# Moving the feed-forward weights of a fused attention and feed-forward kernel from casting DMAs into the queue that loads q, k and v, with staging tiles, on-chip casts and a new issue order

## The chip, the cores and the metric

The kernel runs on one core of a Trainium2 chip. The metric is the device time of one execution in microseconds (us). A profiled execution gives a span 1.7 us shorter than the time; positions such as "at 38.4 us" count from the start of that span. TensorE is called PE in the profile, VectorE DVE, ScalarE ACT, GpSimd POOL, SyncE SP. Every comparison is between runs in the fast state, and each kernel's runs in one call lie within 0.9% of each other.

## The reference, cut to what matters

```python
# q, k, v: (4 batches, 8 heads, 768 positions, 64), float32
k_min, k_max = per chunk of 32 keys, over the chunk
ub   = sum(max(q * k_min, q * k_max))        # bound of each query against each of the 24 chunks
top  = the 6 chunks with the highest bound    # causal chunks only
attn = softmax(q k^T / 8, in those chunks, causal) @ v
x    = attn as (3072 tokens, 512)
h    = x @ w_in                               # w_in 512 x 2048, float32
out  = (h * clip(h + 3, 0, 6) / 6) @ w_out    # w_out 2048 x 512, float32
```

Sixteen head pairs (4 batches, 4 pairs each) go through attention. The tokens of a batch form two groups of 384, and the eight groups go through the two weight matrices. The feed-forward part of a batch needs all four head pairs of that batch, and weights; attention needs no weights.

## The kernel before

Every step is a short function, and one long list of tokens gives the order in which the functions are called. Each engine executes its own instructions in that order. `lk.3` loads the keys of pair 3, `lq` queries, `lv` values, `K`/`Q` transpose keys and queries on PE, `U` are the bounds, `T`/`t8`/`sel`/`L`/`mt` the top-6 selection and its mask, `S` scores, `ex` exponentials, `af` causal masks on GpSimd, `A`/`B` the product with the values, `H` a hidden block (eight matmuls), `O` a quarter of a projection (four matmuls), `xt` DMA transposes of attention output, `Z` warm-up matmuls on zeros, `wi`/`wo` the loads of a quarter of w_in or w_out, `vc` the cast of the values. The other names are copies, casts and reductions between these steps, and the stores.

The loads and the weights, which the change is about:

```python
KS = ring(4, [P, NBLK, 2, D], FP32, "KS")      # the same for QS and VS
PT = [ring(6, [P, 2, 512], BF16, f"PT{i}_") for i in range(3)]
WIN  = const.tile([P, KT, DFF], BF16, name="WIN")
WOUT = const.tile([P, FT, DMODEL], BF16, name="WOUT")

def load(dst, x, i):                            # q, k or v of one pair: two DMAs of 192 KB
    b, hp = divmod(i, NPAIR)
    for e in range(2):
        nc.sync.dma_start(dst[:, :, e, :], x[b, 2 * hp + e].rearrange("(j p) d -> p j d", p=P))

def load_win(c):                                # a DMA that casts fp32 to bf16 on its way
    w = DFF // 4
    nc.gpsimd.dma_start(WIN[:, :, c * w:(c + 1) * w], wi[:, :, c * w:(c + 1) * w])

def load_wout(c):
    nc.gpsimd.dma_start(WOUT[:, 4 * c:4 * c + 4, :], wo[:, 4 * c:4 * c + 4, :])

def cast_v(i):
    nc.gpsimd.tensor_copy(VB[i % 4][:, :, :, 0:D], VS[i % 4][:])
```

The start of the order:

```
PRD PRA lk.0 lq.0 PRP PRL Z.b.10 lv.0 lk.1 lq.2 lq.1 lv.3 lv.2 lk.2 lq.3 lk.3 lv.1 Q.0.a lq.4 rp.0 rn.0 wi.1
qb.0 K.0.b wi.3 lk.4 kb.0 mx.0 wi.2 wi.0 mn.0 vc.0 U.0.c wo.1 lv.4 ub.0 K.1.a wo.0 T.0.x lk.5 kb.1 mx.1 wo.2
Q.2.b t8.0 wo.3 lq.6 rp.2 sel.0 qb.2 mn.1 Q.1.c L.0.y rn.2 lq.5 rp.1 rn.1 qb.1 vc.3 mt.0 U.1.a lv.7 S.0.1.b
... (cut: about 950 more tokens)
```

The softmax here doesn't subtract the row's maximum and nothing guards it: scores larger than these inputs give would overflow.

## Time and profile before

| | before |
|---|---|
| time, median of 3 runs | 325.63 us |
| span of the profiled execution | 323.6 us |
| PE busy | 288.9 us, 89% |
| first score matmul | 38.4 us |
| first hidden matmul | 73.4 us |

The view of stretches (windows) of the kernel before. After the stretch come its length and then, for each engine, busy us and the number of instructions; the last three columns are the granted PE clock (1.00 is full), the share of the DMA engines that was busy (a sum of packet times, which can pass 1), and GB/s moved.

```profile
0.00:10.00 10.00, 7.24 (x22) 3.76 (x22) 4.03 (x16) 2.68 (x4) 8.99 (x19) 1.00 0.99 175
10.00:20.00 10.00, 3.25 (x34) 2.20 (x34) 5.33 (x18) 1.77 (x3) 2.27 (x4) 0.67 1.21 195
20.00:30.00 10.00, 1.51 (x6) 1.14 (x6) 1.36 (x2) 1.34 (x2) 0.00 (x0) 0.50 1.22 196
30.00:40.00 10.00, 4.95 (x51) 3.01 (x53) 1.52 (x3) 2.19 (x4) 1.51 (x2) 0.50 1.26 217
40.00:50.00 10.00, 8.53 (x147) 6.49 (x145) 6.16 (x20) 8.30 (x11) 3.40 (x9) 0.97 1.09 214
...
60.00:80.00 20.00, 18.49 (x320) 13.68 (x319) 13.26 (x35) 16.33 (x21) 9.48 (x20) 1.00 0.78 161
...
120.00:200.00 80.00, 78.89 (x1005) 51.62 (x1002) 49.61 (x144) 56.89 (x75) 19.24 (x43) 1.00 0.35 77
200.00:324.00 124.00, 118.35 (x947) 65.82 (x943) 52.04 (x103) 56.42 (x74) 8.00 (x19) 1.00 0.17 47
```

PE is 17 us busy in the first 40 us, mostly at half clock, and nearly always busy from 60 us on. The DMA engines, on the other hand, are busy all through the first 50 us (shares of 0.99 to 1.26). The head is where PE waits.

PE's timeline in the head, kernel before: start us, duration us, engine, line, operation, output<-input, shapes, count, and in brackets the idle time just before it with what ended it.

```profile
24.59 1.51 PE L236 MATMUL PBb<-IDENT,QS 128*128 128x128 f32 x6 [7.81 <-DMA QS<-in_q_dram]
34.55 1.51 PE L236 MATMUL PBc<-IDENT,QS 128*128 128x128 f32 x6 [8.44 <-DMA QS<-in_q_dram]
35.86 0.45 PE L308 MATMUL PSy<-IDENTB,SEL 96*128 96x96 bf16 x3
38.41 0.39 PE L320 MATMUL PBb<-QB,KB 64*128 64x256 bf16 x2
```

L236 is the transpose of queries. Pair 2's queries arrive at 24.6 and pair 1's at 34.5, each after 8 us of waiting. The line after them, L308, is the mask transpose of pair 0, whose input was finished at 19.7 us; it stands behind the late transposes in PE's order. Only then do the scores (L320) start.

The list of DMA issues on the page of the kernel before (queue, count, KB each, median us from issue to landing):

```profile
QS<-in_q_dram SPq DMA_DIRECT2D x32, 192.0 KB, 3.9
WIN<-in_moe_w_in_dram POOLq DMA_DIRECT2D x4, 512.0 KB, 10.6
WOUT<-in_moe_w_out_dram POOLq DMA_DIRECT2D x4, 512.0 KB, 20.3
```

The size is what is written: 512 KB of bf16 for each 1 MB of fp32 read. Counting the DMA packet records of the trace by queue gives the clearest view of the collision. (This is a count made from the records, in stretches of 4 us; not a view of the profile. Durations are medians; the few 4 B records of each queue are left out of the counts.)

```
kernel before    q, k, v (SyncE queue)                    weights (GpSimd queue)
  4 to  8 us     3376 records of 256 B, 216 GB/s            14 records of 1 KB
 12 to 16 us      610 records,           39 GB/s, 31 ns    612 records, 157 GB/s, 96 ns
 24 to 28 us      626 records,           40 GB/s, 31 ns    607 records, 155 GB/s, 96 ns
 36 to 40 us     3453 records,          221 GB/s             0
```

As long as both queues have work, one record of each alternates. A weight record is four times as large as one of q, k or v and takes three times as long (96 against 31 ns), so equal turns leave q, k and v a fifth of the written bytes.

### The profile page before, as it was taken

Reading aid. Unit: us, or ns where it says so; the run is one execution under the profiler, and the core shown is the slowest. Engines: PE = TensorE matmul, PEld = TensorE weight load, DVE = VectorE, ACT = ScalarE, POOL = GpSimd, SP = SyncE. Lnnn points to the kernel's source line nnn. Section 1 sums busy time; section 2 is a strip of 40 time slices with the busy share of each in tenths; the row PEclk is TensorE's granted clock in tenths of the full one; section 3 lists DMA queues with packets and bytes.
Section 4 is the critical chain, followed back from the end, with each engine's and each line's share of the span. In section 5 each row is a group of like instructions: output and inputs, shape, how many; then the busy total and the mean of one; then the engine's idle time right before and its main releaser. Section 6 shows DMA issues by size and latency. Waiting matters only on the chain.

```text
span 323.6 us, 7386 instructions
## 1 busy us (share of the span) xinstructions
PE 288.9 (89%) x3058; PEld 178.6 (55%) x3058; DVE 168.6 (52%) x435; ACT 180.5 (56%) x234; POOL 61.5 (19%) x133
## 2 busy tenths in 40 slices
...
GB/s 173 193 196 196 223 214 210 218 173 99 49 149 187 120 104 173 137 34 79 146 22 53 34 34 66 49 0 34 67 65 35 50 51 50 66 34 65 2 65 66
DMA packets 92770, 32.21 MB, mean 100 GB/s; under 512 B 85568, under 2 KB 89664, under 8 KB 92736
## 3 DMA queue, kind: packets, MB, share of 16 engines
...
q8 instruction: 24, 0.39, 0.5%
...
## 4 chain that ended last, share of the span: by engine, by line
PE 75%; DMA 7%; DVE 7%; SPq 5%; ACT 4%; issue 1%; DVEq 0%; ACTq 0%
PE PSx L418 13%; PE PSy L418 12%; PE PBc L401 9%; PE PBb L401 8%; PE PBa L401 8%; DMA QS<-in_q_dram 6%; SPq L178 4%; DVE KM L258 4%; PE PSy L357 3%; PE PBa L236 2%; PE PBa L320 2%; PE PBc L320 2%; PE PBb L320 2%; PE PBc L236 2%; ACT KB L252 2%; PE PBa L328 2%
## 5 line engine op out<-in xcount | busy, mean ns | idle before, releaser
L401 PEld LDWEIGHTS <-WIN 128*128 128x128 bf16 x512 | 49.1, 98 | 33.8 <-issue 2.6
L341 POOL TENSOR_SCALAR_AFFINE_SELECT PT<-PT 128x256 bf16<-128x256 bf16 x96 | 38.1, 406 | 155.7 <-ACT PT L334 154.9
L418 PEld LDWEIGHTS <-GT 128*128 128x128 bf16 x384 | 35.8, 98 | 38.9 <-issue 1.1
L418 PE MATMUL PSx<-WOUT,GT 128*128 128x512 bf16 x208 | 49.6, 379 | 0.0
L418 PE MATMUL PSy<-WOUT,GT 128*128 128x512 bf16 x176 | 41.9, 379 | 0.0
L334 ACT ACTIVATE PT<-PBa 128x1024 bf16<-128x1024 f32 (+2 forms) x34 | 32.4, 953 | 4.3 <-PE PBa L328 4.3
L401 PE MATMUL PBc<-XT,WIN 128*128 128x384 bf16 x184 | 33.7, 326 | 1.2 <-DMA XT<-XB 1.2
L401 PE MATMUL PBb<-XT,WIN 128*128 128x384 bf16 x176 | 32.2, 326 | 0.4 <-DVE KM L258 0.4
L334 ACT ACTIVATE PT<-PBb 128x1024 bf16<-128x1024 f32 (+2 forms) x33 | 30.3, 918 | 4.0 <-PE PBb L328 4.0
L334 ACT ACTIVATE PT<-PBc 128x1024 bf16<-128x1024 f32 (+2 forms) x29 | 27.2, 938 | 8.1 <-PE PBc L328 8.1
L412 DVE SCALAR_TENSOR_TENSOR GT<-U,PBb 128x768 bf16<-128x768 bf16 x22 | 20.9, 950 | 16.3 <-PE PSx L418 9.5
L401 PE MATMUL PBa<-XT,WIN 128*128 128x384 bf16 x152 | 27.8, 326 | 0.0
L412 DVE SCALAR_TENSOR_TENSOR GT<-U,PBc 128x768 bf16<-128x768 bf16 x23 | 21.9, 950 | 10.3 <-ACT U L409 10.3
L409 ACT ACTIVATE U<-PBc 128x768 bf16<-128x768 f32 x23 | 18.7, 811 | 14.1 <-PE PBc L401 14.0
L357 PEld LDWEIGHTS <-PT 128*128 128x128 bf16 x672 | 23.9, 97 | 4.5 <-issue 1.2
L328 PEld LDWEIGHTS <-EM 64*128 64x128 bf16 x448 | 22.8, 96 | 5.6 <-issue 0.3
L412 DVE SCALAR_TENSOR_TENSOR GT<-U,PBa 128x768 bf16<-128x768 bf16 x19 | 18.1, 951 | 13.9 <-ACT U L409 13.6
L320 PEld LDWEIGHTS <-KB 64*128 64x128 bf16 x320 | 17.6, 95 | 12.4 <-issue 9.3
L409 ACT ACTIVATE U<-PBb 128x768 bf16<-128x768 f32 x22 | 17.9, 813 | 10.9 <-PE PBb L401 10.4
L409 ACT ACTIVATE U<-PBa 128x768 bf16<-128x768 f32 x19 | 15.4, 812 | 12.4 <-PE PBa L401 12.4
L426 ACT ACTIVATE OT<-PSx 128x512 f32<-128x512 f32 x13 | 7.8, 601 | 23.0 <-PE PSx L418 20.5
L231 POOL CAST VB<-VS 128x768 bf16<-128x768 f32 x16 | 13.1, 829 | 38.4 <-DMA VS<-in_v_dram 26.2
...
## 6 DMA issues: line engine op xcount, KB each, us to landing
KS<-in_k_dram SPq DMA_DIRECT2D x32, 192.0 KB, 4.0
QS<-in_q_dram SPq DMA_DIRECT2D x32, 192.0 KB, 3.9
VS<-in_v_dram SPq DMA_DIRECT2D x32, 192.0 KB, 4.2
...
WIN<-in_moe_w_in_dram POOLq DMA_DIRECT2D x4, 512.0 KB, 10.6
WOUT<-in_moe_w_out_dram POOLq DMA_DIRECT2D x4, 512.0 KB, 20.3
XT<-XB SPq DMA_TRANSPOSE x18, 2.8
```

The source lines that it names most:

```text
L178: nc.sync.dma_start(dst[:, :, e, :], x[b, 2 * hp + e].rearrange("(j p) d -> p j d", p=P))
L231: nc.gpsimd.tensor_copy(VB[i % 4][:, :, :, 0:D], VS[i % 4][:])
L236: nc.tensor.transpose(flat[:, j * P:(j + 1) * P], src[:, j].rearrange("p e d -> p (e d)"), IDENT32[:])
L320: nc.tensor.matmul(PSB[c][:, e, at:at + n], lhsT=K[rows, j * P:(j + 1) * P], rhs=Q[rows, q0:q0 + n], start=True, stop=q0 + n <= Q0, tile_p ...
L328: nc.tensor.matmul(PSB[c][:, e, at + lo - q0:at + hi - q0], lhsT=EM[rows, j, h, :], rhs=M[rows, lo - Q0 - HQ * h:hi - Q0 - HQ * h], start= ...
L334: nc.scalar.activation(PT[i % 3][u][:, :, 0:n], PSB[slot["S", i, u]][:, :, 0:n], ACT.Exp, scale=float(scale))
L341: nc.gpsimd.affine_select(out=T[:, :, lo:lo + P], in_=T[:, :, lo:lo + P], pattern=[[0, 2], [1, P]], compare_op=A.is_ge, fill=0.0, base=0, ...
L357: nc.tensor.matmul(O[:, e, t, :], lhsT=PT[i % 3][u][:, e, lo:lo + P], rhs=VB[i % 4][:, j, e, :], start=(j == 0), stop=(j == qb))
L401: nc.tensor.matmul(PSB[c][:, ff, 0:GRP], lhsT=WIN[:, kt, (2 * f + ff) * P:(2 * f + ff + 1) * P], rhs=XT[g % 3][:, kt, :], start=(kt == 0), ...
L409: nc.scalar.activation(slot["R", g, f][:], PSB[slot["H", g, f]][:, :, 0:GRP], ACT.Relu, bias=3.0)
L412: nc.vector.scalar_tensor_tensor(out=GT[g % 2][:, 2 * f:2 * f + 2, :], in0=slot["R", g, f][:], scalar=6.0, in1=PSB[slot["H", g, f]][:, :, ...
L418: nc.tensor.matmul(PSS[c][:], lhsT=GT[g % 2][:, f, t * P:(t + 1) * P], rhs=WOUT[:, f, :], start=(f == 0), stop=(f == FT - 1))
```

## The change

Its intent: bring the weights in when they are needed and not at the start, and let one queue decide the sequence of everything that is loaded. In the new path a chunk lands as fp32 in one of two staging slots and GpSimd casts it into the weight tile. To find the 16 KB per partition for the slots, the rings of staged q, k, v shrink from 4 to 3 and the tiles of exponentials are cut to the sizes that are used. The whole order is new.

```diff
-    KS = ring(4, [P, NBLK, 2, D], FP32, "KS")
+    KS = ring(3, [P, NBLK, 2, D], FP32, "KS")
     (the same for QS and VS, and in every use of them)
-    PT = [ring(6, [P, 2, 512], BF16, f"PT{i}_") for i in range(3)]
+    PT = [[const.tile([P, 2, sum(x[3] for x in unit)], BF16, name=f"PT{i}_{u}") for u, unit in enumerate(UNITS)]
+          for i in range(3)]
+    WS = ring(2, [P, 4, 512], FP32, "WS")
 
-    def load_win(c): ...        (casting DMA on nc.gpsimd, above)
-    def load_wout(c): ...
+    def load_w(n):
+        c = n % 4
+        nc.sync.dma_start(WS[n % 2][:], wi[:, :, 512 * c:512 * (c + 1)] if n < 4 else wo[:, 4 * c:4 * c + 4, :])
+
+    def cast_w(n):
+        c = n % 4
+        nc.gpsimd.tensor_copy(WIN[:, :, 512 * c:512 * (c + 1)] if n < 4 else WOUT[:, 4 * c:4 * c + 4, :], WS[n % 2][:])

 ORDER (wl = load_w, wc = cast_w)
-PRD PRA lk.0 lq.0 PRP PRL Z.b.10 lv.0 lk.1 lq.2 lq.1 lv.3 lv.2 lk.2 lq.3 lk.3 lv.1 Q.0.a lq.4 rp.0 rn.0 wi.1
-... (cut)
+PRD PRA lk.0 lq.0 PRP PRL Z.b.14 lk.1 lq.1 K.0.a lv.0 kb.0 mx.0 Q.0.b lv.1 mn.0 rp.0 lk.2 rn.0 qb.0 K.1.c lv.2
+U.0.a kb.1 lq.3 Q.1.b ub.0 lk.3 mn.1 T.0.x rp.1 qb.1 t8.0 lq.2 vc.0 lv.3 sel.0 rn.1 L.0.y vc.1 lk.4 mt.0 mx.1
+S.0.1.a S.0.3.b ex.0.1 wl.0 S.0.5.c ex.0.3 af.0.1 lq.4 U.1.a ex.0.5 S.0.4.b af.0.3 ub.1 T.1.x af.0.5 ex.0.4
+wl.1 S.0.0.a vc.2 ...
+... (cut; wl.2 and wl.3 stand beside lk.7 and lq.7, wl.4 to wl.7 in the first feed-forward stage)
```

More of the change, by code (lines that the diff above doesn't have):

```diff
@@ L34 @@
 ORDER = """
-PRD PRA lk.0 lq.0 PRP PRL Z.b.10 lv.0 lk.1 lq.2 lq.1 lv.3 lv.2 lk.2 lq.3 lk.3 lv.1 Q.0.a lq.4 rp.0 rn.0 wi.1
-qb.0 K.0.b wi.3 lk.4 kb.0 mx.0 wi.2 wi.0 mn.0 vc.0 U.0.c wo.1 lv.4 ub.0 K.1.a wo.0 T.0.x lk.5 kb.1 mx.1 wo.2
-Q.2.b t8.0 wo.3 lq.6 rp.2 sel.0 qb.2 mn.1 Q.1.c L.0.y rn.2 lq.5 rp.1 rn.1 qb.1 vc.3 mt.0 U.1.a lv.7 S.0.1.b
-ub.1 S.0.2.c ex.0.1 vc.2 S.0.3.a ex.0.2 S.0.5.b T.1.x af.0.1 lv.6 ex.0.3 S.0.4.c af.0.2 t8.1 ex.0.5 K.2.a
-af.0.3 sel.1 ex.0.4 af.0.5 S.0.0.b lk.6 mn.2 L.1.y kb.2 Q.3.c mx.2 B.0.0.x ex.0.0 lq.7 rn.3 U.2.a rp.3 af.0.0
@@ L40 @@
-mt.1 K.3.b qb.3 ub.2 S.1.2.a lk.7 kb.3 mn.3 S.1.3.c vc.1 ex.1.2 A.0.y mx.3 B.0.1.x lv.5 ex.1.3 na.0 af.1.2
-S.1.0.a S.1.1.b nb.0 T.2.y ex.1.0 af.1.3 U.3.c t8.2 ex.1.1 af.1.0 S.1.4.a ub.3 S.1.5.b af.1.1 ex.1.4 sel.2
-A.1.x L.2.y ex.1.5 Q.4.c na.1 mt.2 af.1.5 T.3.x lq.8 rp.4 rn.4 S.2.0.a qb.4 B.1.0.y t8.3 ex.2.0 S.2.3.b
-S.2.4.c sel.3 ex.2.3 af.2.0 S.2.1.a L.3.x B.1.1.y mt.3 ex.2.4 af.2.3 K.4.b nb.1 ex.2.1 S.3.3.c lk.8 mn.4 kb.4
-af.2.1 S.2.2.a mx.4 A.2.x ex.3.3 na.2 U.4.b ex.2.2 af.3.3 S.2.5.c ub.4 af.2.2 S.3.0.a ex.2.5 T.4.y S.3.5.b
@@ L45 @@
-ex.3.0 t8.4 af.2.5 S.3.4.c B.2.0.x ex.3.5 af.3.0 sel.4 B.2.1.x ex.3.4 af.3.5 L.4.y S.3.1.a nb.2 S.3.2.b ex.3.1
-mt.4 ex.3.2 af.3.1 S.4.5.c S.4.1.a A.3.x ex.4.5 af.3.2 S.4.4.b na.3 ex.4.1 af.4.5 S.4.2.c ex.4.4 X.0.1.y
-af.4.1 X.0.0.x vc.4 xe.0.1 S.4.0.a ex.4.2 S.4.3.b lv.8 xe.0.0 B.3.0.y ex.4.0 af.4.2 B.3.1.y ex.4.3 af.4.0
-H.0.6.c nb.3 af.4.3 A.4.x hu.0.6 H.0.7.a na.4 gt.0.6 K.5.b hu.0.7 H.0.5.c lk.9 mx.5 kb.5 gt.0.7 B.4.0.y hu.0.5
-B.4.1.y mn.5 H.0.4.a nb.4 H.0.2.b gt.0.5 hu.0.4 gt.0.4 H.0.0.c hu.0.2 gt.0.2 H.0.1.a hu.0.0 gt.0.0 X.1.0.x
@@ L50 @@
-hu.0.1 Q.6.b xe.1.0 H.0.3.c lq.10 rp.6 gt.0.1 qb.6 X.1.1.y rn.6 hu.0.3 Q.5.a xe.1.1 vc.7 O.0.0.0.x lq.9 rp.5
-rn.5 H.1.0.b qb.5 lv.11 gt.0.3 vc.6 U.5.a hu.1.0 lv.10 H.1.5.c ub.5 gt.1.0 T.5.y hu.1.5 H.1.2.a t8.5 H.1.6.b
-gt.1.5 hu.1.2 sel.5 H.1.3.c gt.1.2 hu.1.6 gt.1.6 K.7.a hu.1.3 O.0.0.1.x vc.5 lk.11 mx.7 kb.7 O.0.0.2.x lv.9
-mn.7 K.6.b gt.1.3 Q.7.a lk.10 kb.6 mn.6 L.5.y H.1.1.c lq.11 rp.7 mx.6 qb.7 O.0.0.3.x rn.7 hu.1.1 mt.5 U.6.b
-ot.0.0 gt.1.1 vc.8 S.5.5.a st.0.0 ub.6 S.5.3.c lv.12 ex.5.5 S.5.4.b T.6.y ex.5.3 af.5.5 O.1.1.0.x t8.6 ex.5.4
@@ L55 @@
-af.5.3 S.5.1.a S.5.2.c sel.6 ex.5.1 S.5.0.b ex.5.2 H.1.4.a af.5.1 ex.5.0 af.5.2 B.5.0.y hu.1.4 af.5.0 B.5.1.y
-Q.8.c gt.1.4 H.1.7.b lq.12 rp.8 nb.5 qb.8 rn.8 A.5.y hu.1.7 O.1.1.1.x na.5 O.1.1.2.x gt.1.7 L.6.y O.1.1.3.x
-mt.6 S.6.1.a ot.1.1 S.6.2.c S.6.0.b ex.6.1 st.1.1 vc.9 O.1.0.0.y ex.6.2 af.6.1 lv.13 O.1.0.1.y ex.6.0 af.6.2
-S.6.4.a af.6.0 S.6.5.c ex.6.4 S.6.3.b A.6.x ex.6.5 O.1.0.2.y na.6 ex.6.3 af.6.5 O.1.0.3.y af.6.3 K.8.a ot.1.0
-B.6.0.x lk.12 kb.8 mx.8 st.1.0 B.6.1.x K.9.c mn.8 vc.10 U.7.b lk.13 kb.9 nb.6 lv.14 U.8.a mn.9 O.0.1.0.y ub.8
@@ L60 @@
-O.0.1.1.y mx.9 T.8.x ub.7 Q.9.a t8.8 K.11.c lq.13 rp.9 sel.8 O.0.1.2.y lk.15 qb.9 rn.9 L.8.x O.0.1.3.y mt.8
-mx.11 S.8.1.b ot.0.1 S.8.5.a mn.11 T.7.x ex.8.1 st.0.1 O.0.2.0.y ex.8.5 af.8.1 t8.7 S.8.0.b af.8.5 S.8.3.a
-sel.7 ex.8.0 O.0.2.1.y ex.8.3 af.8.0 L.7.x U.9.b mt.7 af.8.3 A.8.x ub.9 S.8.2.a na.8 S.7.3.b ex.8.2 T.9.x
-O.0.2.2.y t8.9 ex.7.3 af.8.2 S.8.4.a af.7.3 sel.9 S.7.5.b ex.8.4 O.0.2.3.y ex.7.5 B.8.0.x B.8.1.x kb.11 af.7.5
-S.7.2.a nb.8 vc.12 ot.0.2 S.7.1.b S.7.4.c ex.7.2 st.0.2 L.9.y O.1.2.0.x mt.9 ex.7.1 af.7.2 ex.7.4 S.9.4.a
@@ L65 @@
-af.7.1 S.9.0.b ex.9.4 S.9.1.c B.7.0.y B.7.1.y ex.9.0 S.9.3.a nb.7 ex.9.1 af.9.0 S.9.5.b O.1.2.1.x xt.3 ex.9.3
-af.9.1 A.9.y ex.9.5 af.9.3 S.9.2.c na.9 af.9.5 S.7.0.a ex.9.2 K.10.b O.1.2.2.x ex.7.0 af.9.2 lk.14 mx.10
-K.12.c kb.10 af.7.0 mn.10 Q.10.a kb.12 mn.12 A.7.y lq.14 rp.10 H.3.4.b vc.11 na.7 qb.10 mx.12 xt.2 B.9.0.y
-lv.15 hu.3.4 B.9.1.y rn.10 H.3.2.c vc.13 gt.3.4 nb.9 H.3.5.a hu.3.2 gt.3.2 H.3.1.b hu.3.5 gt.3.5 H.3.3.c
-hu.3.1 gt.3.1 H.2.6.a hu.3.3 gt.3.3 H.2.2.b hu.2.6 gt.2.6 H.2.4.c hu.2.2 gt.2.2 H.2.3.a hu.2.4 gt.2.4 H.2.7.b
@@ L70 @@
-hu.2.3 gt.2.3 H.2.0.c hu.2.7 gt.2.7 H.2.5.a hu.2.0 gt.2.0 H.2.1.b hu.2.5 gt.2.5 U.10.c hu.2.1 Q.12.a ub.10
-gt.2.1 T.10.y rp.12 Q.11.c t8.10 qb.12 H.3.6.b lq.15 rp.11 sel.10 qb.11 O.1.2.3.x rn.12 hu.3.6 L.10.y rn.11
-U.12.a ot.1.2 mt.10 st.1.2 U.11.c gt.3.6 O.2.2.0.x ub.11 ub.12 T.11.y S.10.1.b t8.11 S.10.4.c ex.10.1 S.10.5.a
-ex.10.4 S.10.2.b af.10.1 sel.11 O.2.2.1.x ex.10.5 L.11.y ex.10.2 O.2.2.2.x af.10.5 mt.11 S.11.0.c af.10.2
-S.11.3.a ex.11.0 S.11.5.b O.2.2.3.x ex.11.3 af.11.0 T.12.y S.10.3.c ex.11.5 af.11.3 t8.12 S.11.2.a ot.2.2
@@ L75 @@
-af.11.5 S.10.0.b ex.10.3 sel.12 st.2.2 O.2.1.0.x ex.11.2 af.10.3 L.12.y O.2.1.1.x mt.12 ex.10.0 af.11.2
-B.10.0.y B.10.1.y af.10.0 S.12.1.c nb.10 S.12.2.a ex.12.1 S.12.3.b ex.12.2 af.12.1 S.12.0.c O.2.1.2.x ex.12.3
-af.12.2 O.2.1.3.x ex.12.0 af.12.3 S.12.4.a ot.2.1 af.12.0 S.12.5.b S.11.1.c ex.12.4 st.2.1 A.10.y A.12.x na.10
-vc.14 ex.12.5 Q.15.a na.12 ex.11.1 Q.13.b af.12.5 qb.15 af.11.1 B.12.0.y rn.13 A.11.x rp.13 H.3.0.c na.11
-qb.13 xt.4 K.13.b hu.3.0 B.12.1.y mx.13 kb.13 O.2.0.0.x gt.3.0 O.2.0.1.x mn.13 O.2.0.2.x nb.12 O.2.0.3.x
@@ L80 @@
-O.3.2.0.y ot.2.0 H.4.2.c st.2.0 H.4.3.b hu.4.2 gt.4.2 O.3.0.0.x hu.4.3 O.3.0.1.x gt.4.3 O.3.0.2.x U.13.c
-H.4.1.b ub.13 rp.15 rn.15 H.4.7.c hu.4.1 gt.4.1 H.3.7.a hu.4.7 gt.4.7 H.4.5.b hu.3.7 gt.3.7 H.4.4.c hu.4.5
-gt.4.5 O.3.0.3.x hu.4.4 H.4.0.a gt.4.4 ot.3.0 st.3.0 T.13.x hu.4.0 H.4.6.b t8.13 O.3.2.1.y sel.13 hu.4.6
-gt.4.0 L.13.x O.3.2.2.y mt.13 gt.4.6 S.13.3.c S.13.2.a ex.13.3 S.13.4.b O.4.0.0.x ex.13.2 af.13.3 O.3.2.3.y
-ex.13.4 af.13.2 S.13.1.c S.13.5.a ot.3.2 S.11.4.b ex.13.1 st.3.2 O.4.1.0.y ex.13.5 af.13.1 ex.11.4 O.4.1.1.y
@@ L85 @@
-af.13.5 O.4.1.2.y O.4.1.3.y K.15.c ot.4.1 K.14.a kb.15 mx.15 st.4.1 O.4.2.0.y kb.14 mn.15 O.4.2.1.y mn.14
-O.4.2.2.y mx.14 U.15.b S.13.0.c ub.15 O.4.2.3.y ex.13.0 O.4.0.1.x ot.4.2 af.13.0 st.4.2 T.15.y O.4.0.2.x t8.15
-O.4.0.3.x sel.15 Q.14.a ot.4.0 B.13.0.y rp.14 rn.14 st.4.0 L.15.x B.13.1.y qb.14 mt.15 U.14.b nb.13 S.15.4.c
-ub.14 S.15.0.a ex.15.4 S.15.3.b T.14.x ex.15.0 O.3.1.0.y t8.14 ex.15.3 O.3.1.1.y af.15.0 sel.14 O.3.1.2.y
-af.15.3 O.3.1.3.y B.11.0.x ot.3.1 B.11.1.x st.3.1 S.15.1.c nb.11 vc.15 S.15.2.a ex.15.1 L.14.y xt.5 S.15.5.b
@@ L90 @@
-ex.15.2 af.15.1 mt.14 A.13.x S.14.5.c ex.15.5 af.15.2 na.13 S.14.4.a ex.14.5 af.15.5 S.14.1.b A.15.y ex.14.4
-af.14.5 B.15.0.x na.15 S.14.0.c ex.14.1 S.14.2.a ex.14.0 af.14.1 S.14.3.b B.15.1.x ex.14.2 af.14.0 H.5.2.c
-nb.15 ex.14.3 af.14.2 H.5.3.a hu.5.2 af.14.3 gt.5.2 B.14.0.y hu.5.3 H.5.6.b gt.5.3 B.14.1.y hu.5.6 H.5.4.c
-nb.14 gt.5.6 xt.7 H.5.5.a hu.5.4 gt.5.4 H.5.1.b hu.5.5 gt.5.5 H.5.7.c hu.5.1 gt.5.1 A.14.x hu.5.7 H.5.0.a
-na.14 gt.5.7 xt.6 H.7.0.b hu.5.0 gt.5.0 H.7.2.c hu.7.0 O.5.0.0.y hu.7.2 O.5.0.1.y H.7.5.a O.5.2.0.x hu.7.5
@@ L95 @@
-O.5.2.1.x O.5.2.2.x O.5.2.3.x O.5.0.2.y ot.5.2 O.5.0.3.y st.5.2 O.5.1.0.x ot.5.0 O.5.1.1.x st.5.0 gt.7.0
-O.5.1.2.x gt.7.2 O.5.1.3.x gt.7.5 H.7.3.b ot.5.1 st.5.1 H.7.4.c hu.7.3 gt.7.3 H.7.1.a hu.7.4 gt.7.4 H.7.6.b
-hu.7.1 gt.7.1 H.7.7.c hu.7.6 gt.7.6 O.7.1.0.y hu.7.7 O.7.1.1.y gt.7.7 O.7.0.0.x O.7.0.1.x O.7.0.2.x O.7.0.3.x
-O.7.1.2.y ot.7.0 O.7.1.3.y st.7.0 H.6.6.a ot.7.1 st.7.1 H.6.7.b hu.6.6 gt.6.6 H.6.3.c hu.6.7 gt.6.7 H.6.1.a
-hu.6.3 gt.6.3 H.6.5.b hu.6.1 gt.6.1 H.6.4.c hu.6.5 gt.6.5 H.6.0.a hu.6.4 gt.6.4 H.6.2.b hu.6.0 gt.6.0
@@ L100 @@
-O.7.2.0.x hu.6.2 O.6.0.0.y gt.6.2 O.7.2.1.x O.7.2.2.x O.7.2.3.x O.6.0.1.y ot.7.2 O.6.0.2.y st.7.2 O.6.0.3.y
-O.6.2.0.x ot.6.0 O.6.2.1.x st.6.0 O.6.2.2.x O.6.2.3.x O.6.1.0.y ot.6.2 O.6.1.1.y st.6.2 O.6.1.2.y O.6.1.3.y
-ot.6.1 st.6.1
+PRD PRA lk.0 lq.0 PRP PRL Z.b.14 lk.1 lq.1 K.0.a lv.0 kb.0 mx.0 Q.0.b lv.1 mn.0 rp.0 lk.2 rn.0 qb.0 K.1.c lv.2
+U.0.a kb.1 lq.3 Q.1.b ub.0 lk.3 mn.1 T.0.x rp.1 qb.1 t8.0 lq.2 vc.0 lv.3 sel.0 rn.1 L.0.y vc.1 lk.4 mt.0 mx.1
+S.0.1.a S.0.3.b ex.0.1 wl.0 S.0.5.c ex.0.3 af.0.1 lq.4 U.1.a ex.0.5 S.0.4.b af.0.3 ub.1 T.1.x af.0.5 ex.0.4
@@ new lines @@
+wl.1 S.0.0.a vc.2 t8.1 S.0.2.c lv.4 ex.0.0 K.2.b sel.1 lv.5 ex.0.2 Q.3.a af.0.0 mn.2 L.1.y rp.3 A.0.x af.0.2
+lk.5 rn.3 qb.3 K.3.c mt.1 lq.6 mx.2 kb.2 S.1.0.a kb.3 B.0.0.y mx.3 lk.6 S.1.3.b ex.1.0 mn.3 B.0.1.y ex.1.3
+Q.2.a af.1.0 na.0 U.3.c lq.5 rp.2 af.1.3 nb.0 vc.3 S.1.2.b qb.2 ub.3 ex.1.2 rn.2 T.3.x lv.6 S.1.5.c t8.3 U.2.a
+af.1.2 ex.1.5 S.1.1.b sel.3 S.1.4.c af.1.5 ex.1.1 ub.2 L.3.y ex.1.4 K.4.b af.1.1 mt.3 wc.0 S.3.0.a lk.7 mn.4
+kb.4 S.3.3.c B.1.0.x ex.3.0 mx.4 T.2.y B.1.1.x ex.3.3 t8.2 af.3.0 wl.2 S.3.5.a S.3.1.b Q.4.c ex.3.5 af.3.3
@@ new lines @@
+sel.2 ex.3.1 S.3.4.a af.3.5 lq.7 nb.1 rp.4 af.3.1 A.1.y rn.4 wc.1 L.2.x qb.4 S.3.2.b na.1 ex.3.4 U.4.c mt.2
+A.3.y ex.3.2 ub.4 S.2.3.a vc.4 wl.3 na.3 S.2.1.c S.2.2.b ex.2.3 af.3.2 lv.7 T.4.x vc.5 B.3.0.y ex.2.1 t8.4
+S.2.5.a ex.2.2 af.2.3 lv.8 B.3.1.y af.2.1 S.2.4.c sel.4 ex.2.5 af.2.2 K.5.b nb.3 ex.2.4 af.2.5 S.2.0.a lk.8
+mn.5 L.4.x kb.5 B.2.0.y Q.6.c mx.5 ex.2.0 B.2.1.y lq.9 rn.6 rp.6 af.2.0 nb.2 K.6.b qb.6 mt.4 X.1.0.y lk.9 kb.6
+mn.6 S.4.1.a S.4.4.c ex.4.1 xe.1.0 A.2.x ex.4.4 af.4.1 Q.5.a mx.6 X.1.1.y lq.8 rp.5 rn.5 U.6.c vc.6 qb.5 na.2
@@ new lines @@
+U.5.b ub.6 lv.9 S.4.0.a ub.5 S.4.3.c ex.4.0 xe.1.1 T.5.x H.1.3.b t8.5 ex.4.3 af.4.0 H.1.2.a af.4.3 sel.5
+hu.1.3 gt.1.3 wc.2 L.5.y X.0.0.x hu.1.2 S.4.5.c mt.5 xe.0.0 S.5.5.b ex.4.5 A.4.y gt.1.2 X.0.1.x ex.5.5 af.4.5
+S.5.1.c wl.4 na.4 S.5.2.a ex.5.1 af.5.5 S.5.3.b xe.0.1 ex.5.2 af.5.1 S.5.4.c T.6.y ex.5.3 H.0.1.a af.5.2 t8.6
+wc.3 ex.5.4 H.0.3.b sel.6 hu.0.1 gt.0.1 H.0.0.c af.5.3 wl.5 hu.0.3 vc.7 gt.0.3 H.1.7.a lv.10 hu.0.0 gt.0.0
+H.0.7.b hu.1.7 gt.1.7 B.5.0.x hu.0.7 S.4.2.c H.1.4.a gt.0.7 ex.4.2 af.4.2 S.5.0.b hu.1.4 H.1.0.c ex.5.0 gt.1.4
@@ new lines @@
+B.5.1.x af.5.0 hu.1.0 Q.7.b nb.5 A.5.y lq.10 rp.7 gt.1.0 H.1.6.a qb.7 rn.7 vc.9 H.0.4.c hu.1.6 na.5 lv.12
+gt.1.6 H.0.2.b hu.0.4 gt.0.4 H.0.5.a wc.4 hu.0.2 gt.0.2 K.7.c hu.0.5 L.6.x B.4.0.y lk.10 mx.7 kb.7 B.4.1.y
+wc.5 H.0.6.b gt.0.5 wl.6 nb.4 H.1.5.a hu.0.6 mn.7 vc.8 wl.7 O.0.2.0.y mt.6 hu.1.5 gt.0.6 lv.11 O.0.2.1.y
+gt.1.5 S.6.0.c S.6.1.b S.6.3.a ex.6.0 O.0.0.0.x ex.6.1 af.6.0 U.7.c ex.6.3 af.6.1 S.6.5.b ub.7 af.6.3 S.6.2.a
+ex.6.5 S.6.4.c O.0.0.1.x ex.6.2 af.6.5 Q.8.b ex.6.4 af.6.2 K.8.a wc.6 lq.11 rn.8 rp.8 H.1.1.c mn.8 qb.8 lk.11
```

68 lines of the change are left out of this document (54 added, 14 removed).

## The prediction

> **What bounds the kernel now.** TensorE, except in the first 38 us. The windows view gives PE 17 us busy in the first 40 us (mostly at a granted clock of 0.5), and 272 us busy in the 284 us after that at clock 1.00: from there only some 12 us are to be won, 4 of them the tail. The head is what can move. There the waits name DMA: Q.2's transposes wait for QS 7.8 us (start 24.6), Q.1's 8.4 us (start 34.5), and pair 0's mask transpose, whose SEL was ready at 19.7, stands behind them in PE's order until 35.7. The first score matmul starts at 38.4, the first hidden matmul at 73.4.
>
> The reason is the weights. GpSimd issues all eight chunks between 5 and 12 us. The DMA packet records show that queue writing 156 GB/s from about 9 to 34 us, while the SyncE queue, which carries q, k and v, falls from about 200 GB/s to 39. The Trainium skill, "DMA: Bandwidth & Descriptors", "Queues, rings and completion order", says each DMA engine round-robins by packet between queues with work; the trace agrees: 628 weight packets beside 630 of q/k/v per 4 us, at 96 ns against 18 to 30.
>
> **What changes.** Removed: eight casting DMAs and their 6.2 us of issue on GpSimd. Added: eight 1 MB fp32 loads in the SyncE queue and eight GpSimd casts of 128x2048, 2.2 us each if scaled from the 829 ns of the 128x768 cast, 17.7 us on an engine 19% busy. Moved: weights to where they are needed. Rings of 3 instead of 4 only limit how far loads run ahead. PE's work stays, apart from four more warm-up matmuls (1.7 us, while it waits anyway).
>
> **Cost.** At 196 to 215 GB/s one load (two 192 KB DMAs) takes 1.9 us; a weight chunk, 512 packets of 2 KB at the 84 ns of the 2 KB output stores, over 16 engines, 2.7 us, say 3. Summed in the new order: k0 lands near 4.4, q1 10, q3 20, q2 23, k4 27, the first weights 30, q5 47, the fourth weights 59. Head, with durations from the trace: warm-up to 7.5, K.0 and Q.0 to 10.5, bounds to 13.5, top-8 and select to 17.8, mask to 18.9: first scores at 19 instead of 38.4, 19.4 us earlier. PE has 1.1 us more work left then. At the old pace all later loads arrive ahead of use: first hidden matmul near 57 (its weights cast near 38), the fourth chunk needed near 68, cast by 61. I allow 1.3 us for casts standing before causal masks. All of the gain is on the critical path: 325.6 - 19.4 + 1.1 + 1.3 = 308.6 us.
>
> **What would show it.** First score matmul near 19, first hidden matmul at 53 to 60; no QS wait over 3 us; no packets on the software queue; q/k/v at about 200 GB/s up to 25 us; DMA share over 0.9 until about 60 us, under 0.6 later; PE near 97% from 20 us on; casts of 2.0 to 2.5 us.
>
> **What would make it wrong.** Weight chunks taking much over 3 us, or SyncE blocked in order on a ring or staging slot, so that hidden matmuls wait for WIN; casts delaying masks and so PE; the new order packing PE worse. Better if the early attention packs tighter than before.
>
> I predict 308.6 us, 8 in 10 between 302 and 315; faster by over 2%: 0.95, within 2%: 0.04, slower: 0.01.

## More of the kernel before

The clock column has a trap: the clock records of this trace begin at 9.9 us, and the view counts the time before them as 1.00. The durations say otherwise: a 128x512 warm-up matmul took 634 ns there, against 379 ns for matmuls of that size later.

## The result, and the profile after

The kernel after takes 306.51 us (median of 4 runs, 306.18 to 306.98) against 325.74 us of the kernel before in the same rounds. The ratio is 0.9403, with a 95% interval of 0.9366 to 0.9439. Ratios in this document are formed from the fast runs of a kernel and of the kernel before in the same rounds, so they are not quite the ratio of the medians quoted.

| | before | after |
|---|---|---|
| time, median | 325.74 us | 306.51 us |
| span | 323.6 us | 304.5 us |
| PE busy | 288.9 us | 282.3 us |
| first score matmul | 38.4 us | 14.7 us |
| first hidden matmul | 73.4 us | 57.7 us |
| POOL busy | 61.5 us | 69.8 us |

The same stretches of the kernel after:

```profile
0.00:10.00 10.00, 7.37 (x44) 3.89 (x44) 5.29 (x18) 2.84 (x4) 4.37 (x13) 1.00 1.03 183
10.00:20.00 10.00, 6.84 (x93) 4.04 (x89) 5.79 (x22) 6.05 (x8) 3.65 (x6) 0.83 1.35 219
20.00:30.00 10.00, 8.03 (x139) 6.23 (x135) 7.87 (x24) 8.39 (x12) 3.12 (x7) 1.00 1.09 260
30.00:40.00 10.00, 8.97 (x160) 6.60 (x160) 8.27 (x35) 7.54 (x10) 5.80 (x10) 1.00 1.07 257
40.00:50.00 10.00, 8.51 (x171) 6.66 (x168) 6.87 (x25) 8.49 (x10) 4.92 (x9) 1.00 1.14 219
...
60.00:80.00 20.00, 20.00 (x223) 13.49 (x222) 14.82 (x33) 15.74 (x21) 10.07 (x14) 1.00 1.05 256
...
120.00:200.00 80.00, 76.88 (x863) 48.98 (x867) 46.63 (x115) 50.98 (x66) 15.06 (x33) 1.00 0.34 81
200.00:324.00 124.00, 97.87 (x781) 55.38 (x789) 42.90 (x90) 50.32 (x66) 7.07 (x18) 0.99 0.11 36
```

PE is 31.2 us busy in the first 40 us instead of 17.0, and at full clock for most of them. The DMA share shows the other half: the engines stay saturated until 80 us (1.05 in the stretch from 60 to 80 us, against 0.78 before), because the weights are spread over that time.

PE's timeline in the head, kernel after (L239 is the transpose of keys or queries, L311 the mask transpose of pair 0, L323 the scores):

```profile
5.96 0.82 PE L239 MATMUL PBa<-IDENT,KS 128*128 128x128 f32 x6
8.28 0.85 PE L239 MATMUL PBc<-IDENT,KS 128*128 128x128 f32 x6 [0.85 <-DMA KS<-in_k_dram]
11.01 0.87 PE L239 MATMUL PBb<-IDENT,QS 128*128 128x128 f32 x6 [0.28 <-ACT QB L258]
14.48 0.30 PE L311 MATMUL PSy<-IDENTB,SEL 96*128 96x96 bf16 x3 [2.26 <-DVE SEL L301]
14.71 0.28 PE L323 MATMUL PBa<-QB,KB 64*128 64x256 bf16 x2
```

The waits of 8 us are gone; the longest wait for a load is 0.85 us. Transposes take 0.82 to 0.87 us instead of 1.51, because the clock is up.

The DMA issues on the page of the kernel after:

```profile
QS<-in_q_dram SPq DMA_DIRECT2D x32, 192.0 KB, 4.0
WS<-in_moe_w_in_dram SPq DMA_DIRECT2D x4, 1024.0 KB, 8.2
WS<-in_moe_w_out_dram SPq DMA_DIRECT2D x4, 1024.0 KB, 7.7
```

The fp32 chunks have 8 us from issue to landing, but nothing stands still for them: no line of PE's or DVE's waits names WS, WIN or WOUT as a late DMA. The weight casts, from the view of the staging tile (count; min/median/max in ns; first and last start):

```profile
L197 POOL CAST WIN<-WS x4: 1889/1889/1889, 33.3 to 64.8; 128x2048 bf16<-128x2048 f32 x4
L197 POOL CAST WOUT<-WS x4: 1890/1893/1894, 77.7 to 95.4; 128x2048 bf16<-128x2048 f32 x4
```

Where the 19.1 us of the span came from, from the gaps between PE's records: PE's idle time before the first score matmul fell from 23.0 to 5.2 us (17.8 gained); PE's busy time fell by 6.5 us (288.89 to 282.35); the tail is 0.3 us shorter; but idle time after the first score matmul rose from 7.6 to 13.2 us (5.5 lost). Two of these terms need a correction. The trace after shows 3036 matmuls beside 3062 weight loads, so 26 records are missing, and the gaps that they leave (25 between projection matmuls, L421, all put down to "issue") add up to 1.8 us, which counts as idle and not as busy. The trace of e3 below, the same order of compute with all its records, has none of these gaps. So busy time really fell by about 4.8 us, which I put down chiefly to the head no longer running at half clock (argued, not tested apart), and about 3.8 us of new idle time are real. Most of that is PE waiting for the DMA transposes of X: the view of the XT tile puts it at 1.2 us before and 4.4 us after.

### The profile page after: what moved, and what is told of

Same layout as the page of the kernel before. It is cut to its first block, busy times and chain, and to the rows that moved or that the text cites. A ratio compares the mean times of both kernels' runs of the same rounds, so it can differ in the third digit from the quotient of the medians.

```text
span 304.5 us, 7383 instructions
## 1 busy us (share of the span) xinstructions
PE 282.3 (93%) x3036; PEld 176.0 (58%) x3062; DVE 168.0 (55%) x435; ACT 181.5 (60%) x234; POOL 69.8 (23%) x133
## 4 chain that ended last, share of the span: by engine, by line
PE 77%; DVE 9%; ACT 5%; DMA 2%; SPq 2%; issue 2%; DVEq 0%; ACTq 0%
PE PSy L421 14%; PE PSx L421 10%; PE PBa L404 10%; PE PBb L404 9%; PE PBc L404 8%; DVE KM L261 4%; DMA XT<-XB 2%; SPq L386 2%; PE PBb L323 2%; PE PSx L360 2%; PE PSy L360 2%; PE PBc L323 2%; PE PBb L239 2%; ACT KB L255 2%; PE PSx L292 2%
## 5 line engine op out<-in xcount | busy, mean ns | idle before, releaser
L404 PEld LDWEIGHTS <-WIN 128*128 128x128 bf16 x512 | 49.1, 98 | 37.9 <-issue 5.1
L421 PEld LDWEIGHTS <-GT 128*128 128x128 bf16 x384 | 35.8, 98 | 38.2 <-issue 0.9
L421 PE MATMUL PSy<-WOUT,GT 128*128 128x512 bf16 x205 | 51.6, 379 | 1.1 <-issue 0.2
L421 PE MATMUL PSx<-WOUT,GT 128*128 128x512 bf16 x153 | 37.1, 379 | 0.7 <-issue 0.5
L404 PE MATMUL PBa<-XT,WIN 128*128 128x384 bf16 x192 | 35.1, 326 | 1.7 <-DMA XT<-XB 1.6
L415 DVE SCALAR_TENSOR_TENSOR GT<-U,PBa 128x768 bf16<-128x768 bf16 x24 | 22.8, 950 | 21.7 <-ACT U L412 21.5
L337 ACT ACTIVATE PT<-PBc 128x1024 bf16<-128x1024 f32 (+2 forms) x33 | 30.7, 932 | 2.3 <-PE PBc L331 2.2
L412 ACT ACTIVATE U<-PBa 128x768 bf16<-128x768 f32 x24 | 19.5, 814 | 20.5 <-PE PBa L404 20.3
L337 ACT ACTIVATE PT<-PBa 128x1024 bf16<-128x1024 f32 (+2 forms) x30 | 26.8, 893 | 6.4 <-PE PBa L331 6.2
L404 PE MATMUL PBc<-XT,WIN 128*128 128x384 bf16 x152 | 27.8, 326 | 0.3 <-DMA XT<-XB 0.3
L323 PEld LDWEIGHTS <-KB 64*128 64x128 bf16 x320 | 16.5, 94 | 13.4 <-issue 10.4
L415 DVE SCALAR_TENSOR_TENSOR GT<-U,PBc 128x768 bf16<-128x768 bf16 x19 | 18.1, 952 | 10.5 <-ACT U L412 10.4
L297 DVE MAX8 T<-PSx 96x8 f32<-96x32 f32 x156 | 16.5, 178 | 7.7 <-PE PSx L292 7.6
L234 POOL CAST VB<-VS 128x768 bf16<-128x768 f32 x16 | 13.2, 827 | 27.3 <-PE PSy L360 18.3
```

What stands on the lines that cost most here:

```text
L234: nc.gpsimd.tensor_copy(VB[i % 4][:, :, :, 0:D], VS[i % 3][:])
L297: nc.vector.max(out=T8[i % 2][:, s, :], in_=view[:, s, :])
L323: nc.tensor.matmul(PSB[c][:, e, at:at + n], lhsT=K[rows, j * P:(j + 1) * P], rhs=Q[rows, q0:q0 + n], start=True, stop=q0 + n <= Q0, tile_p ...
L337: nc.scalar.activation(PT[i % 3][u][:, :, 0:n], PSB[slot["S", i, u]][:, :, 0:n], ACT.Exp, scale=float(scale))
L404: nc.tensor.matmul(PSB[c][:, ff, 0:GRP], lhsT=WIN[:, kt, (2 * f + ff) * P:(2 * f + ff + 1) * P], rhs=XT[g % 3][:, kt, :], start=(kt == 0), ...
L412: nc.scalar.activation(slot["R", g, f][:], PSB[slot["H", g, f]][:, :, 0:GRP], ACT.Relu, bias=3.0)
```

## The experiments

Theory A: the gain is that q, k and v no longer share the DMA engines with the weights in the head. Rival B: the new order of compute and loads is the gain. Rival C: the path is (fp32 through one queue in a fixed sequence). Rival D: the warm-ups and the clock are. All runs below gave correct results unless it is said.

### e1: the new order, with the weights early again

```diff
 (kernel after; load_w issues the casting DMA of the kernel before on nc.gpsimd, cast_w is not called, WS stays unused)
-... lk.2 rn.0 qb.0 K.1.c ...
+... lk.2 rn.0 wl.1 wl.3 wl.2 wl.0 wl.5 wl.4 wl.6 wl.7 qb.0 K.1.c ...
-(wl.0 to wl.7 and wc.0 to wc.7 at their places)
```

> The kernel after, with its new order of compute and of q, k and v loads, its rings of 3 and its 14 warm-ups, but all eight weight chunks are again casting DMAs issued by GpSimd at about 5 to 12 us, straight into the weight tiles (no staging, no casts). Theory A (the gain is q, k and v no longer sharing the DMA engines with the weights in the head): the weight queue again runs from about 9 to 34 us and q, k, v fall to about 40 GB/s; first scores may still start early (k0, q0, k1, q1 land first) but pair 2's keys (third k load) land near 36 instead of 16, and the time is 317 to 325 us. Rival B (the new order is what helps): 305 to 309 us.

Measured: 327.22 us, ratio 1.0032 (0.9995 to 1.0069). All of the gain is gone. It is 2.2 us above theory A's range and far from rival B's. The timeline of PE in this run shows where the new order stops:

```profile
15.06 1.51 PE L238 MATMUL PBb<-IDENT,QS 128*128 128x128 f32 x6 [3.39 <-DMA QS<-in_q_dram]
37.94 1.51 PE L238 MATMUL PBb<-IDENT,KS 128*128 128x128 f32 x6 [12.40 <-DMA KS<-in_k_dram]
41.49 1.51 PE L238 MATMUL PBa<-IDENT,QS 128*128 128x128 f32 x6 [2.04 <-DMA QS<-in_q_dram]
```

The first scores still start at 19.5 us, since the first loads are out before the weights, but the keys of pair 2 then come at 37.9 us, after a wait of 12.4 us. The weight records run from 8 to 34 us at 157 GB/s as in the kernel before, with q, k, v at 39. The new order alone is worth nothing while the weights are early.

### e2: the old order, with the weights late

```diff
 (kernel before)
-... rn.0 wi.1 qb.0 K.0.b wi.3 ... wi.2 wi.0 ... wo.1 ... wo.0 ... wo.2 Q.2.b t8.0 wo.3 ...
+... af.0.5 wi.3 wi.2 ... af.1.5 wi.1 wi.0 ... af.3.5 wo.0 wo.1 ... vc.7 wo.2 wo.3 ...
```

> The kernel before, with its order, rings of 4 and 10 warm-ups, with one thing moved: the eight casting DMAs of GpSimd stand later in GpSimd's order (two after pair 0's causal masks, two after pair 1's, two after pair 3's, two after the cast of v of pair 7). Theory A: first scores at 16 to 20 us instead of 38.4, time 304 to 310 us. Rival B (order): 322 to 327 us.

Measured: 309.06 us, ratio 0.9471 (0.9435 to 0.9508). Eight tokens moved in the old kernel, with its casting DMAs and without staging tiles, give 17 of the 19 us. The timeline of PE:

```profile
15.18 1.49 PE L232 MATMUL PBb<-IDENT,QS 128*128 128x128 f32 x6
16.46 1.21 PE L232 MATMUL PBc<-IDENT,QS 128*128 128x128 f32 x6
21.40 0.40 PE L316 MATMUL PBb<-QB,KB 64*128 64x256 bf16 x2
```

The two query transposes that waited 8 us each now follow each other at 15.2 and 16.5 us without a wait. (Moving the tokens also takes 6.2 us of DMA issue out of GpSimd's head. That this was what held PE is ruled out by the waits of the kernel before: up to 39 us none of PE's names GpSimd.) The scores start at 21.4, a little later than the 16 to 20 that was expected; the time is inside the range.

### e3: the new order, late weights by casting DMAs

```diff
 (kernel after; load_w as in e1, no casts)
+... af.0.2 wl.0 wl.1 ... af.3.2 wl.2 wl.3 ... vc.7 wl.4 wl.5 ... vc.9 wl.6 wl.7 ...
```

> The kernel after with its order, but the weights come by casting DMAs of GpSimd at about the times at which the SyncE queue moves them in the kernel after (near 23, 47, 67 and 84 us, two at each), with no staging tile and no casts. Theory A (when the weights move is what counts, not by which queue or in which type): 304 to 309 us, with 15 us of GpSimd casts gone and nothing gained from it. Rival C (the fp32 path through the same queue in a fixed sequence is what helps): at least 6 us slower than the kernel after, so over 312 us.

Measured: 307.12 us, ratio 0.9419 (0.9383 to 0.9456), the same as the kernel after within the noise. Its issues fell at 23.3, 43.8, 67.1 and 78.4 us. Rival C falls: neither the fp32 staging nor the single queue is needed for the gain. The reverse holds too: the 15 us of casts that the change put on GpSimd cost nothing that can be seen, since taking them away gains nothing (GpSimd issues the casting DMAs again in e3, 6.1 us, and its busy time still falls from 69.8 to 60.8 us). While these late weights moved, q, k and v again fell to 40 GB/s (28 to 32 us), but by then the loads that PE needed next were already there.

### e4: half of the weights late, old order

```diff
 (kernel before; the four wi tokens stay where they are)
-... wo.1 ... wo.0 ... wo.2 ... wo.3 ...
+... af.3.5 wo.0 wo.1 ... vc.7 wo.2 wo.3 ...
```

> The kernel before with only the four w_out chunks moved late (two after pair 3's causal masks, two after the cast of v of pair 7); the four w_in chunks stay at 5 us. A dose test. Theory A: half of the weights hold the DMA engines for about half as long (9 to about 21 us), so first scores near 27 us and a time near 315 us (311 to 319). Rival B: 322 to 327 us.

Measured: 315.77 us, ratio 0.9685 (0.9643 to 0.9727), first scores at 28.3 us. PE's timeline:

```profile
22.94 1.51 PE L232 MATMUL PBb<-IDENT,QS 128*128 128x128 f32 x6 [6.12 <-DMA QS<-in_q_dram]
28.28 0.28 PE L316 MATMUL PBb<-QB,KB 64*128 64x256 bf16 x2
```

Eight early chunks put the first scores at 38.4 us, four at 28.3, none at 21.4; the times are 325.9 (the kernel before in these rounds), 315.8 and 309.1 us. Half of the dose takes away 60% of the harm. One us of delay of the first scores costs about one us of time: (325.9 - 315.8) / (38.4 - 28.3) is 1.00, and (315.8 - 309.1) / (28.3 - 21.4) is 0.97. In the old order, the delay of the head passes into the total in full.

### e5, e6, e9: the warm-ups

The first transposes take 0.82 us in the kernel after and 1.51 in the kernel before, and the kernel after has 14 warm-up matmuls instead of 10. I formed the theory that the four more warm-ups raise the clock in time, and tested it three ways, each with one token changed.

```diff
 e5 (kernel after):   -Z.b.14  +Z.b.10
 e6 (kernel before):  -Z.b.10  +Z.b.14
 e9 (e2):             -Z.b.10  +Z.b.14
```

> The kernel after with 10 warm-up matmuls instead of 14. The head came out 4.2 us better than I predicted, and the trace gives the reason as the clock: granted 1.0 from 5.0 us on in the kernel after, only from 9.9 us in the kernel before. Clock theory (the four more warm-ups keep TensorE busy long enough for the clock to be raised before the first transposes): first transposes take 1.5 us again instead of 0.8, the first score matmul moves from 14.7 to 17 or 18 us, time 308 to 310.5 us. Rival (the clock rises because the data comes earlier, the warm-ups do nothing): 306 to 307 us.

> The kernel before with 14 warm-up matmuls instead of 10, nothing else. Theory A (its head is bound by the late q loads): first score matmul stays at 38.4 us within 0.5, time 325 to 326.5 us. Rival D (a good part of the gain is the warm-ups and the clock): 322 us or less.

> The kernel before with the late weights of e2 and also 14 warm-ups. It tells what of the 2.6 us between e2 (309.1) and the kernel after (306.5) is the warm-ups and what is the new order. Clock theory: the first transposes at full clock, first scores 1.5 to 3 us earlier than e2's 21.4, time 306 to 308 us. If the warm-ups do nothing here either: 309 us.

Measured: e5 305.47 us, ratio 0.9336 (0.9290 to 0.9382); e6 325.96 us, ratio 0.9966 (0.9923 to 1.0009); e9 308.76 us, ratio 0.9434 (0.9391 to 0.9477). None of the three is told from its partner (0.9403, 1, 0.9471) in the direction that the clock theory needs. It fell. PE's timeline of e5:

```profile
5.54 1.41 PE L239 MATMUL PBa<-IDENT,KS 128*128 128x128 f32 x6
6.79 0.82 PE L239 MATMUL PBb<-IDENT,QS 128*128 128x128 f32 x6
14.88 0.28 PE L323 MATMUL PBa<-QB,KB 64*128 64x256 bf16 x2
```

The traces say why: with 10 warm-ups the first transpose of e5 does run at half clock (1.41 us), but it starts at 5.5 us instead of 6.0, and the second ends at 7.6 against 7.4 us; the first scores start at 14.9 us against 14.7. In these traces, what the warm-ups give to the clock they take in time. A second profile of the kernel after (the control e14 below), with 14 warm-ups, has the first scores at 14.9 us too, so the difference of 0.2 us is no more than one kernel shows. And e4, with 10 warm-ups, had its first transpose at 0.85 us where the kernel before, with the same 10 and nearly the same start (6.55 against 6.44 us), had 1.51. (The record of the kernel after has the clock at 1.0 from 4.6 us, not the 5.0 of the expectation of e5.) Rival D falls as well: e6 leaves the first scores at 39.5 us, even 1.1 later than before, in a head that waits for loads.

### e7, e12, e13: the waits for the DMA transposes

The result had left 5.5 us of new PE idle time, and its largest named part was XT. e7 fills the two longest of those waits with other work.

```diff
 e7 (kernel after)
-O.3.2.0.x ... O.3.2.1.x ... H.5.2.a ... H.5.7.b ... O.3.2.2.x ... H.4.7.c ... H.5.0.a ... O.3.2.3.x
+O.3.2.0.x ... O.3.2.1.x O.3.2.2.x O.3.2.3.x ... H.5.2.a ... H.5.7.b ... H.4.7.c ... H.5.0.a
-B.14.1.x O.5.2.3.y nb.14 af.15.0 S.15.3.b ot.5.2 S.15.5.a ex.15.3 st.5.2 S.15.4.c A.15.x O.5.0.0.y ... na.15 ... xt.6 ...
+B.14.1.x nb.14 af.15.0 S.15.3.b S.15.5.a ex.15.3 A.15.x ex.15.5 S.15.4.c af.15.3 na.15 O.5.2.3.y xt.6 ot.5.2 ...
 (O.5.0 now accumulates in x, B.15 in y)
```

> The kernel after, with its two longest TensorE waits for the DMA transposes of X filled with other work: two projections moved ahead of the first hidden matmul of group 5, and in the last batch the low value matmuls of pair 15 moved two score units earlier, with one projection put after them. Those waits are 1.64 us at 197 and 1.69 us at 259. If they are on the critical path as the chain of waits says: 303 to 305 us, and XT waits of TensorE of about 1.5 us in sum instead of 4.4. If something else catches them: 306 us or more.

Measured: 306.81 us, ratio 0.9387 (0.9342 to 0.9433): nothing gained. The timelines of PE at the hidden matmuls show where it went. First the kernel after, then e7:

```profile
197.24 1.46 PE L404 MATMUL PBa<-XT,WIN 128*128 128x384 bf16 x8 [1.64 <-DMA XT<-XB]
201.17 1.46 PE L404 MATMUL PBc<-XT,WIN 128*128 128x384 bf16 x8 [0.31 <-DMA XT<-XB]
259.02 1.46 PE L404 MATMUL PBb<-XT,WIN 128*128 128x384 bf16 x8 [1.69 <-DMA XT<-XB]
```

```profile
198.06 1.46 PE L401 MATMUL PBa<-XT,WIN 128*128 128x384 bf16 x8 [0.55 <-DMA XT<-XB]
201.94 1.46 PE L401 MATMUL PBc<-XT,WIN 128*128 128x384 bf16 x8 [1.12 <-DMA XT<-XB]
265.08 1.46 PE L401 MATMUL PBa<-XT,WIN 128*128 128x384 bf16 x8 [1.28 <-DMA XT<-XB]
```

The wait of 1.64 us became 0.55, but the next hidden matmuls, of the other group of the same batch, now wait 1.12 us instead of 0.31; and the wait at 259 is gone, but the next group waits 1.28 us at 265. SyncE issues these transposes one after the other, three to a group (six in 8.3 us from 192 us on in e7), so PE only came to the second group earlier than its transposes did. e12 therefore also puts more of the first group's work before the second group's:

```diff
 e12 (e7)
-H.5.2.a H.5.7.b H.4.7.c H.5.0.a H.4.5.c H.4.2.a H.5.1.b H.4.3.c    (hu and gt likewise; other tokens between them)
+H.5.2.a H.5.7.b H.5.0.c H.5.1.a H.4.7.c H.4.5.a H.4.2.b H.4.3.c
-H.6.5.b H.6.7.a H.6.0.c H.6.2.b H.7.5.a H.7.7.c H.7.0.b H.6.1.a
+H.6.5.b H.6.7.a H.6.0.c H.6.2.b H.6.1.a H.7.7.c H.7.0.b H.7.5.a
 e13 (e12)
-S.1.0.a kb.3 B.0.0.y mx.3 lk.6 S.1.3.b ex.1.0 mn.3 B.0.1.y
+B.0.0.y B.0.1.y S.1.0.a kb.3 mx.3 lk.6 S.1.3.b ex.1.0 mn.3
```

> The kernel after, unchanged, as the control of this call: 306 to 307 us, or the same ratio of about 0.940 to the kernel before.

> e7 took the two longest XT waits away and won nothing; its trace shows TensorE waiting for the next DMA transposes instead (1.12 us at 201 for those of group 4, 1.28 us at 264 for those of group 7). Here four hidden matmuls of group 5 instead of two stand before the first of group 4, and one more of group 6 before the first of group 7. If those follow-up waits were what caught e7's gain: 303 to 305 us, at least 1.5 us under the control of this call. If the end is held by something else (the issue of the transposes in sequence, or the chain behind it): within 0.7 us of the control.

> e12, and the 1.24 us wait of TensorE at 23.5 us (scores of pair 1 wait for the cast of q of pair 3) filled with 1.08 us of pair 0's value matmuls that stood just after it. If that wait is on the critical path: 0.5 to 1 us under e12. If it is caught by the next wait as in e7: the same as e12 within 0.3.

Measured in the same five rounds: the control 306.78 us, ratio 0.9428 (0.9399 to 0.9457); e12 304.16 us, ratio 0.9340 (0.9314 to 0.9367); e13 304.17 us, ratio 0.9345 (0.9322 to 0.9367). e12 is 2.6 us below the control and the intervals do not overlap; it beats both kernels. From the first score matmul to the end of the span it takes 287.5 us against 289.6 of the control and 290.3 of e7. (Its profiled execution, 305.22 us, is the slowest of its five.) PE's idle time after the first score matmul is 10.5 us against 12.9 of the control, and its waits for XT are 1.1 us against 4.1. The waits of PE in e12 that name XT (engine, tile, line, what it waited for: us in total, times, longest):

```profile
PE PBb L401 <- DMA XT<-XB: 1.1, 2, 0.9
```

They sum to 1.1 us in two waits, the longer of them at 124 us, in an earlier batch; the ones that e7 showed at 201 and 264 us are gone. How much each of the two reorderings gave was not tested apart. e13 came out the same as e12 in time: the wait at 23.5 us can be filled, but what PE does next then waits. Its trace shows 0.62 us at 24.0 and 1.02 us at 26.9 us for the 1.24 us that was filled. Here the chain runs through ACT and DVE, and PE's gap was slack.

### e11: rings of three in the old kernel, a failed experiment

```diff
 (kernel before)
-KS = ring(4, ...)   KS[i % 4]      (QS and VS likewise)
+KS = ring(3, ...)   KS[i % 3]
```

> The kernel before with rings of 3 instead of 4 for the staged q, k and v, nothing else: what the memory for the staging tile costs. I said it only limits how far loads run ahead: the same as the kernel before within 1 us. Rival (the rings matter in the head): over 2 us slower.

Measured: 345.61 us, and a wrong result. In the old order the load of pair 3 (`lk.3`) stands before the transpose of pair 0 (`K.0`), so with three slots it overwrites the keys of pair 0 before they are used, and the first transposes wait until 36.5 us for loads that they should not need. The number says nothing about what a ring of 3 costs. It only says that the depth of a ring and the order are one decision: the new order, made for 3, never lets a load run past its third predecessor's use. The opposite experiment, the kernel after with rings of 4, did not build, because the tiles no longer fit on the chip beside the staging slots. What the ring's depth costs by itself stays open.

## Why the prediction was right

Predicted 308.6 us (302 to 315), measured 306.51. Point by point:

- **The cause.** That the weights starve q, k and v in the first 35 us, and that moving them is the gain: shown from both sides. With the weights early again the new kernel loses everything (e1), with the weights late the old one gains 17 us (e2), half of the weights give about half (e4). The Trainium skill's page "DMA: Bandwidth & Descriptors", in "Issuing engines are not separate DMA queues", says that DMAs from different engines run on the same 16 DMA engines and interleave. The trace of the kernel before agrees with it: from 12 to 16 us the two queues wrote 39 and 157 GB/s side by side, together no more than the 216 of q, k and v alone. e3 and the kernel after fit it too: 307.1 and 306.5 us with two queues and with one.
- **The head, the mis-sized term.** I put the first scores at 19 us and a gain of 19.4 us there; they came at 14.7, so 23.7 us. I had taken durations from a head that ran largely at half clock. Against the 18.9 us of the prediction's sum it is 4.2 us: 3.1 had arisen by the end of the second transpose (10.5 predicted, 7.4 measured: warm-ups done at 6.1 instead of 7.5, two transposes in 1.5 us instead of 3.0), 0.5 from there to the end of the mask (7.9 us instead of 8.4), and 0.6 because the first score matmul does not wait for the mask (14.7 against 15.3 us). The Trainium skill's page "TensorE: Matmul & The Clock Gate", in "What's actually happening", describes a clock of half or full rate, set by activity in free-running windows of 3413 ns. The clock records agree: in the kernel before 1.0 for 3.413 us, then 0.5 for 27.3 us (8 times that), then 1.0; in the kernel after 0.5 for only 3.4 us. The durations came from the first 10 us, which the view marks 1.00 for want of clock records. I should have compared them with the same instruction later in the trace: a set of six transposes takes 1.51 us there and 0.87 at 42 us.
- **From first scores to the first hidden matmul.** I predicted 38 us and it took 43; so the first hidden matmul came at 57.7 us, inside the 53 to 60 that I gave, through two errors that cancel. PE idles 6.2 us in that stretch (4.6 in the kernel before) and is busy for 36.8 us of it (30.4 before): among other work, the keys, queries and bounds of pairs 5 and 6 stand there in the new order.
- **PE near 97% from 20 us on: wrong.** It was 80 to 90% busy from 20 to 60 us. The kernel before had 85% in the same stage, in the windows that I quoted from; the figure I gave was that of the later stages.
- **DMA share under 0.6 after 60 us: wrong.** It was 1.05 from 60 to 80 us. I forgot the four w_out chunks, which this order issues at 67 and 85 us. It cost nothing there: PE was busy for all 20 us of that stretch.
- **The casts.** 1.89 us each, under the 2.2 estimated and just under the 2.0 to 2.5 given as a sign. The 1.3 us allowed for causal masks behind casts did not show: e3 has no casts and is no faster.
- **No weight packets on the software queue, no query wait over 3 us:** both as said. The allowance that was not made is the 3.2 us more that PE waits for XT, which ate most of what the head gave beyond the prediction. e12 takes about 2 us of it back.
- **The number, in part luck.** The head gave 4.3 us more than predicted. From the first scores to the end the kernel after took 289.8 us against 285.2, so 4.6 us more where the sum allowed 2.4 (1.1 of work, 1.3 for the casts). The work was right, about 1.1 us with the missing records counted in; the rest is idle time that the prediction did not have. The two errors cancel down to 2.1 us.

How much the new order is worth once the weights are late is best read from e2 and e3, which ran in the same rounds, both with casting DMAs: 309.06 us (308.18 to 309.24) and 307.12 us (306.66 to 307.87). The runs do not overlap, so the new order gives nearly 2 us there, with its rings of three and 14 warm-ups included and the weights not at quite the same times. It has its first scores 6.1 us earlier (15.3 against 21.4) but gives most of that back: PE waits 4.4 us for XT in e3 and not at all in e2.

## What to carry to other kernels

Before tuning an order of compute, count what each DMA queue moves in the stretch where the critical engine waits: a prefetch that nobody needs for 40 us was the whole 17 us, and that it stood in another engine's queue did not make it harmless. Judge a late load by when it is needed and not by the queue that it stands in; moving eight tokens did nearly all that a new path and a new schedule did. And when a wait is filled and nothing is gained, look at the next wait for the same slow producer before giving up: filling the second one as well gave 2.6 us against the control.

## What the Trainium skill lacked or had wrong

- "DMA: Bandwidth & Descriptors", "Queues, rings and completion order": it gives round-robin by packet, and speaks of packets of several descriptors. It does not say what that does to two queues with packets of different size. Here records of 256 B and of 1 KB written (2 KB read) alternated one for one (610 beside 612 in 4 us), which left the small ones 39 of 196 GB/s; alone they had 216.
- The same page, "DMA Transpose (X-bar)": the section gives no time for the issue of one transpose on SyncE between on-chip tiles (the page's one on-chip figure is in cycles, for 8,192 tiles, in a table about a later chip). Here, in the kernel after, a 128x512 bf16 one occupied the queue for 1.19 to 1.52 us and landed a median of 2.5 us after its issue, and three or six of them in sequence were what PE waited for.
- "TensorE: Matmul & The Clock Gate": its clock windows and the variation from run to run agree with the traces (spells of 3.413 us and multiples; with one and the same head the clock rose at 4.6 us in the kernel after, at 5.1 in its repeat e14 and at 7.3 in e12). Its account could add that more warm-up matmuls are no gain in themselves: with 14 instead of 10 the first scores came at 14.7 and 14.9 us instead of 14.9 in the kernel after, and at 39.5 instead of 38.4 us in the kernel before, with no difference in time beyond the noise in either.
